# Sparse attention and soft mixture of experts on one core: sampled block numbers packed three to a word, taken apart in registers

## The chip, the cores and the metric

The kernel runs on one core of a Trainium2 chip. The metric is the device time of one execution in microseconds (us); lower is better. The core's engines are called PE (TensorE; PEld is its weight load), DVE (VectorE), ACT (ScalarE), POOL (GpSimd) and SP (SyncE, which here only issues transfers). Each has a sequencer of its own, which reads the instruction stream, runs register and semaphore instructions itself and hands the others to the engine's queue; the profile writes POOLq or ACTq for what a sequencer does.

## The reference

Four batches with eight heads attend over 768 positions of 64 numbers each. Positions come in 24 blocks of 32. A query block sees its own block and the two neighbours, the first and the last block, and three more blocks whose numbers are data (`sampled_blocks`, 24 rows of three numbers from 0 to 23); query blocks 0 and 23 see everything. The output, as 3072 rows of 512, goes through a soft mixture of eight experts with four slots each.

```python
mask = np.abs(blk_i - blk_j) <= window
mask = mask | (blk_i == 0) | (blk_j == 0) | (blk_i == n_blocks - 1) | (blk_j == n_blocks - 1)
for qb in range(n_blocks):
    for kb in sampled_blocks[qb]:
        mask[qb * block:(qb + 1) * block, kb * block:(kb + 1) * block] = True
scores = np.where(mask, scores, -1000000000.0)
...
return np.matmul(attn, v).astype(np.float32)
```

After it: `logits = x @ phi`, a softmax over rows that gathers slots, two matrix products per expert with a maximum between them, and a softmax over slots that spreads the results back to the rows.

## The kernel before, in words

Attention comes first, up to about 247 us of the profiled execution, then the experts. All work of the attention part is a list of tasks (class `Plan`, line 129). A task has an engine or a choice of engines with a cost, the tasks that it needs, and the buffers that it takes. The order in which all tasks are emitted is written out by hand (`ORDER`, line 67), and each engine runs its tasks in that order. Costs and due times written beside the tasks serve to choose where some instructions stand: `run` (line 209) calls a task's `pre` function, which loads its register values, 1.6 us of planned time ahead of the engine's current task, and `hold` (line 241) ties paced transfers, among them the late expert weights, to instructions of PE.

Batches run one after another. In a batch the query blocks 0 and 23 are "dense" (`plan_dense`, line 847); the other 22 go in pairs (`plan_pair`, line 624), 11 pairs to a batch. For one pair:

- K is staged for each of the two query blocks (`stage_k`, line 536) into one of four `kst` tiles of 256 columns. `fixed` copies the three neighbouring blocks (line 553, POOL) and, where the tile is new to the batch, the first and the last block (line 551, POOL). `sampled_` (line 555) copies the three sampled blocks, three instructions on ACT (line 559) or POOL (line 564); their source address in `ktile` is `ds(t.vals[j] * BLK, BLK)`, with a register value in it.
- V is staged in the same way (`stage_v`, line 573) into one of six `vrs` tiles, three copies (line 586, POOL; line 584, ACT for the last pairs). Their source address is `ds(t.vals[j], 1)`.
- q is scaled by 1/8 (lines 603 and 605). PE multiplies q with the staged K (line 643, tile `s`, 64 matmuls for a pair). DVE takes row maxima (line 663, `nm`), ACT the exponentials (line 668, `p`), DVE turns them (line 675, `ptt`). For each two pairs PE multiplies with V (line 741, `av`, from V itself and from `vrs`), and DVE divides by the row sums (lines 734 to 736, tile `x`). Dense blocks do the same at lines 864 (`sd`), 882, 895, 899 and 741 (`avd`).
- Groups of four such tiles are turned on PE (line 957, `mxt`) and go through the logits (line 1008, `ml`) and the slot sums (line 1092, `ms`).

The sampled numbers reach the engines so. `index_load` (line 351) brings `sampled_blocks` into `scr` by a transfer on ACT's queue. `sreg_copy` (line 470) has DVE copy the low words into `sreg`, an int32 tile of 24 rows with three numbers, for K. `index_math` (line 359) computes on DVE, in float32, `vreg`, the same shape for V: a number's position in V, or an empty position where the block is already seen by the mask or is a repeated one. `block_numbers` (line 439) loads the numbers of a pair of rows, `t[0:1, 2 * j + 1:2 * j + 3, :]`, with one load instruction on the engine that will copy (line 443), keeps the six register values by batch, pair, engine and largest value, and hands each row its three. The steps from a register value to an address (times the block's stride, times four bytes, plus the tile's base) run on the same engine's sequencer just before the copy, as one fused register instruction. `sreg` and `vreg` are made early: the tasks `t_sreg` and `t_vreg` (lines 491 and 492) stand ahead of the first pair.

After attention come the expert products (line 1507, then 1515) and the spreading of the result (line 1609), with expert weights arriving by transfers on SP's queue.

Of the kernel before, what the change touches and what calls it, by code (L numbers as in the profile page):

```python
# [12 lines left out]
I32 = mybir.dt.int32  # L13
F32R = mybir.dt.float32r
AF = mybir.ActivationFunctionType
ALU = mybir.AluOpType
# [4 lines left out]
BLK, NB, NR = 32, 24, 3  # L21
# [94 lines left out]
E_ = mybir.EngineType  # L116
# [12 lines left out]
class Plan:  # L129
# [6 lines left out]
    def add(self, f, opts, deps, key, acq=(), byte=0, pre=None, pace=False, kind=None, mode=None, ni=0,  # L136
            turn=False):
        t = Task(f, opts if isinstance(opts, list) else [opts], deps, key, acq, byte, pre, pace,
                 kind, mode, ni, turn)
        self.tasks.append(t)  # L140
        return t
# [106 lines left out]
def attn_moe_kernel(ctx, tc, qT, kT, vfull, vtab, sampled, phi, w1, w2, out):  # L248
    nc = tc.nc
    PE, ACT, DVE, POOL, SP = nc.tensor, nc.scalar, nc.vector, nc.gpsimd, nc.sync  # L250

    const = ctx.enter_context(tc.tile_pool(name="const", bufs=1))
# [16 lines left out]
    for k in RUNS:  # L269
        o = (at - NW // 2) * P * WP  # L270
# [71 lines left out]
    ssum = const.tile([P, 1], F32, name="ssum")  # L342


    sreg = const.tile([1, NB, NR], I32, name="sreg")

    vreg = const.tile([1, NB, NR], I32, name="vreg")

    scr = pw.tile([P, DM], F32, tag="x", name="scr", bufs=XB)

    def index_load():
# [4 lines left out]
        )  # L356
        return sraw

    def index_math():
        o = NB * NR * 2  # L360
        own, dup, tmp, iot = (scr[0:1, o + k * NB * NR:o + (k + 1) * NB * NR]
                              .rearrange("p (i j) -> p i j", i=NB) for k in range(4))
        DVE.tensor_copy(out=own, in_=sreg)
        POOL.iota(iot, pattern=[[1, NB], [0, NR]], base=0, channel_multiplier=0,
                  allow_small_or_imprecise_dtypes=True)
        POOL.memset(vbuf[1][:, VH:2 * VH], 0.0)
        DVE.tensor_single_scalar(out=dup, in_=own, scalar=0.0, op=ALU.is_equal)
        DVE.scalar_tensor_tensor(out=dup, in0=own, scalar=float(NB - 1), in1=dup,
                                 op0=ALU.is_equal, op1=ALU.max)
        DVE.tensor_tensor(out=tmp, in0=own, in1=iot, op=ALU.subtract)  # L370
        DVE.tensor_tensor(out=tmp, in0=tmp, in1=tmp, op=ALU.mult)
        DVE.scalar_tensor_tensor(out=dup, in0=tmp, scalar=1.0, in1=dup,
                                 op0=ALU.is_le, op1=ALU.max)
        for j in range(1, NR):
            for k in range(j):
                DVE.tensor_tensor(out=tmp[:, :, j], in0=own[:, :, j], in1=own[:, :, k], op=ALU.is_equal)
                DVE.tensor_tensor(out=dup[:, :, j], in0=dup[:, :, j], in1=tmp[:, :, j], op=ALU.max)
        DVE.tensor_scalar(out=tmp, in0=own, scalar1=-1.0, scalar2=float(NB), op0=ALU.mult, op1=ALU.add)
        DVE.tensor_tensor(out=tmp, in0=tmp, in1=dup, op=ALU.mult)
        DVE.scalar_tensor_tensor(out=vreg, in0=own, scalar=-1.0, in1=tmp, op0=ALU.add, op1=ALU.add)  # L380


    att = ExitStack()
# [4 lines left out]
    ktile, vtile = [None] * B, [None] * B  # L388
# [6 lines left out]
    for n in range(NVR):  # L395
        n = (B * (NB - 2) + n) % NVR
# [40 lines left out]
    both = {}  # L437

    def block_numbers(b, t, i, eng, most):
        j = (i - 1) // 2  # L440
        key = b, most, j, eng
        if key not in both:
            _, both[key] = nc.values_load_multi_w_load_instructions(  # L443
                t[0:1, 2 * j + 1:2 * j + 3, :], engines=[{"ACT": E_.Activation, "POOL": E_.Pool}[eng]], min_val=0, max_val=most,
                skip_runtime_bounds_check_because="block numbers lie in range by the definition of the input")
        o = (i - 2 * j - 1) * NR
        return both[key][o:o + NR]

# [20 lines left out]

    def sreg_copy(t):  # L470
        sraw = scr[0:1, 0:NB * NR * 2].bitcast(I32).rearrange("p (i j w) -> p i j w", i=NB, j=NR)
        DVE.tensor_copy(out=sreg, in_=sraw[0:1, :, :, 0])

    fills = Rec()

# [13 lines left out]
    t_warm = add(warm, ("PE", 3.0), [], -41, acq=[("s", use)], mode="F", ni=12)  # L489
    use.append(t_warm)  # L490
    t_sreg = add(sreg_copy, ("DVE", 0.3), [t_idx], -39)
    t_vreg = add(lambda t: index_math(), ("DVE", 4.0), [t_sreg], -38)


# [41 lines left out]
    def stage_k(b, i, n, use):  # L536
        k = nst[0] % NKST
        nst[0] += 1
        new = fresh.get(k) != b
        fresh[k] = b  # L540
        z = Rec()
        w, r0 = (0, 96) if i % 2 else (32, 0)

        def fixed(t):
            kv = ktile[b]
            k = took[0] % NKST
            took[0] += 1
            z.st = st = kst[k]
            if filled.get(k) != b:
                filled[k] = b  # L550
                POOL.tensor_copy(out=st[:, :, 128:192].rearrange("p c (g s) -> p c g s", g=2),
                                 in_=kv.rearrange("p c (g s) -> p c g s", g=NB)[:, :, 0:NB:NB - 1, :])
            POOL.tensor_copy(out=st[:, :, w:w + 96], in_=kv[:, :, (i - 1) * BLK:(i + 2) * BLK])  # L553

        def sampled_(t):
            for j, o in enumerate((r0, 192, 224)):
                st, src = z.st, ktile[b][:, :, ds(t.vals[j] * BLK, BLK)]
                if t.eng == "ACT":
                    x = ACT.activation(out=st[:, :, o:o + BLK], in_=src, func=AF.Copy, scale=1.0)  # L559
                    while opening:  # L560
                        tc.add_manual_dep(x.ins, opening.pop().ins.name, mybir.DependencyInfo(
                            mybir.DependencyClass.Sync, mybir.DependencyReason.DATA), reason="first")
                else:
                    POOL.tensor_copy(out=st[:, :, o:o + BLK], in_=src)  # L564

        f = add(fixed, ("POOL", 0.95 if new else 0.52), [t_k[b]], n - 4, acq=[("kst", use)], kind="fix")
        r = add(sampled_, [("ACT", 0.72), ("POOL", 0.86)], [f, t_sreg], n - 2.5,
                pre=lambda e: block_numbers(b, sreg, i, e, NB - 1), kind="smp")
        k_use[b].extend([f, r])
        use.extend([f, r])  # L570
        return z, r

    def stage_v(b, i, n, use):
        z = Rec()

        def copies(t):
            st = vrs[nvs[0] % NVR]
            nvs[0] += 1
            z.st = st.rearrange("p a j (r d) -> p a j r d", r=2)
            vf = vtile[b].rearrange("p a k r d -> p a k (r d)")  # L580
            for j in range(NR):
                o, src = st[:, :, j:j + 1, :], vf[:, :, ds(t.vals[j], 1), :]
                if t.eng == "ACT":
                    ACT.activation(out=o, in_=src, func=AF.Copy, scale=1.0)
                else:
                    POOL.tensor_copy(out=o, in_=src)  # L586

        v = add(copies, [("POOL", 1.12), ("ACT", 1.4)] if n >= len(items) - 2 else ("POOL", 1.12), [t_v[b], t_vreg], n - 1, acq=[("vrs", use)],
                pre=lambda e: block_numbers(b, vreg, i, e, NB), kind="vst")
        v_use[b].append(v)  # L590
        use.append(v)
        return z, v
# [31 lines left out]
    def plan_pair(b, g, n):  # L624
# [5 lines left out]
        for r in range(2):  # L630
            use = []
            kd.append(stage_k(b, 2 * g + 1 + r, n, use))
            ku.append(use)
# [613 lines left out]
    for gi in range(6):  # L1247
        Ts = done[4 * gi:4 * gi + 4]
        t_m, k = plan_group(gi, Ts, Ts[-1][0])
# [7 lines left out]
    m, n = NPRE, first[B - 1]  # L1257
# [24 lines left out]
    for j in range(NPT):  # L1282
        add(lambda t, m=m + j: load_w(m, turned), ("SP", 0.47), [qks[N - 2]], N + j / 10, acq=[("ptt", end_use)], byte=4 * WP * P,
            kind="lw", pace=0.4)
# [8 lines left out]
    def load_halves(m, tag, nb):  # L1293
# [8 lines left out]
        kind="lx", pace=0.4)  # L1302
# [60 lines left out]
    for j, g in enumerate((0, 1, 2, 5)):  # L1363
        t_n = plan_combine(g, N - 4 + j)

        n, b_use = N + 2 + j, []
# [171 lines left out]
    for n in range(2 * NE):  # L1538
        hf, e = n // NE, n % NE
# [174 lines left out]
```

## Time and profile before

| | us |
|---|---|
| median of 3 runs | 302.05 (301.56 to 302.61) |
| profiled execution, its own time | 300.76 |
| span of the profiled execution, first to last instruction | 298.9 |
| busy PE / DVE / POOL / ACT in it | 266.8 / 212.2 / 182.1 / 158.6 |
| mean granted TensorE clock, share of full speed | 0.98 |

The profile is of one execution. Times in its rows count from the start of the span. A row of instructions gives engine, line, operation, what is written and read (out<-in), a count, and in square brackets how long the engine had been idle and what ended that ("issue": nothing that the profile shows). In the chain, "POOLq L443" is time of POOL's sequencer on line 443. Register, semaphore and load instructions of a sequencer do not count as busy time of its engine.

### The profile page before, as it was taken

What the parts mean: (1) busy time and instruction counts of PE and PEld (TensorE: products, weight loads), DVE (VectorE), ACT (ScalarE), POOL (GpSimd) and SP (SyncE); (2) the same over time, 40 slices, a digit from 0 to 9 for tenths busy, and PEclk for the clock granted to TensorE, in tenths of its full rate; (3) what the DMA queues carried; (4) which work ended last, traced back from release to release, by engine and by line L of the source; (5) the groups of instructions that cost most, each with busy time, mean ns of one, the idle gap of its engine ahead of it and who ended that gap; (6) DMA issues with size and microseconds to landing.
All of it is one profiled execution on the core that took longest, in us unless ns stands there. A gap on an engine that the chain in (4) does not pass through costs nothing.

```text
span 298.9 us, 17524 instructions
## 1 busy us (share of the span) xinstructions
PE 266.8 (89%) x7221; PEld 190.3 (64%) x7221; DVE 212.2 (71%) x485; ACT 158.6 (53%) x482; POOL 182.1 (61%) x523
## 2 busy tenths in 40 slices
PE   7699998989999999999989999999887899999940
PEld 4458675876877676777666685867656663355530
DVE  6698895878998968989896889997676223012450
ACT  4866775763674975576877643556464122001340
POOL 5749789798847799785898968587953013000000
PEclk9989997999999999999999999999999999999996
DMA  7935663430364861034575220778669999999998
GB/s 252 405 119 163 193 185 95 148 81 22 89 202 138 214 182 42 24 108 134 179 207 162 72 77 19 236 225 240 220 192 303 397 380 409 422 420 409 342 306 280
DMA packets 30546, 61.96 MB, mean 207 GB/s; under 512 B 4481, under 2 KB 17922, under 8 KB 29314
## 3 DMA queue, kind: packets, MB, share of 16 engines
q1 hardware_dynamic: 30320, 60.70, 61.2%
q8 instruction: 57, 0.93, 1.3%
q14 instruction: 23, 0.19, 0.2%
q10 hardware_dynamic: 146, 0.13, 0.1%
HBM read 54.52 MB, written 6.29 MB: 203 GB/s over the span
## 4 chain that ended last, share of the span: by engine, by line
PE 55%; DVE 19%; issue 8%; POOL 5%; ACT 4%; POOLq 3%; ACTq 1%; DMA 1%; DVEq 0%
PE av L741 22%; PE s L643 7%; PE pso L1515 5%; DVE ptt L675 5%; PE pf L1507 5%; DVE nm L663 5%; PE mxt L957 3%; ACT p L668 3%; PE sd L864 3%; PE ml L1008 2%; DVE x L736 2%; POOLq L443 2%; POOL vrs L586 2%; PE avd L741 2%; DVE ptd L899 2%
## 5 line engine op out<-in xcount | busy, mean ns | idle before, releaser
L586 POOL COPY vrs<-v 128x260 f32 x258 | 91.8, 404 | 22.4 <-issue 10.5
L668 ACT ACTIVATE p<-s,nm 128x256 f32<-128x256 f32 x176 | 71.2, 478 | 29.0 <-DVE nm L663 21.5
L741 PE MATMUL av<-v,ptt 64*64 64x130 f32 (+2 forms) x1728 | 77.1, 282 | 2.8 <-issue 2.7
L741 PEld LDWEIGHTS av<-v,ptt 64*64 64x64 f32 (+2 forms) x1728 | 53.6, 131 | 24.2 <-issue 17.7
L675 DVE STREAM_TRANSPOSE ptt<-p 128x512 f32<-128x512 f32 x88 | 57.5, 688 | 8.8 <-ACT p L668 8.3
L663 DVE TENSOR_REDUCE nm<-s 128x2 f32<-128x512 f32 x88 | 54.9, 680 | 3.5 <-PE s L643 3.2
L643 PE MATMUL s<-kst,q 64*32 64x256 f32 x1408 | 47.7, 387 | 4.7 <-POOL kst L553 2.5
L553 POOL COPY kst<-ktile 128x384 f32<-128x384 f32 x88 | 42.9, 507 | 13.6 <-PE s L643 10.8
L741 PE MATMUL av<-vrs,ptt 64*32 64x130 f32 x2112 | 43.8, 277 | 5.2 <-issue 2.5
L741 PEld LDWEIGHTS av<-vrs,ptt 64*32 64x32 f32 x2112 | 36.0, 106 | 10.8 <-issue 3.7
L643 PEld LDWEIGHTS s<-kst,q 64*32 64x32 f32 x1408 | 28.2, 107 | 15.2 <-POOL vrs L586 3.2
L559 ACT ACTIVATE kst<-ktile 128x128 f32 x135 | 30.6, 310 | 12.9 <-PE s L643 8.2
L564 POOL COPY kst<-ktile 128x128 f32 x129 | 32.7, 293 | 4.4 <-issue 2.3
L895 ACT ACTIVATE pd<-sd,nb 128x384 f32<-128x384 f32 x32 | 16.7, 577 | 16.4 <-DVE nb L890 16.2
L741 PE MATMUL avd<-v,ptd 64*64 64x130 f32 x768 | 23.1, 271 | 0.0
L741 PEld LDWEIGHTS avd<-v,ptd 64*64 64x64 f32 x768 | 21.7, 132 | 1.6 <-PE s L643 0.8
L456 ACT COPY xT<-mxt 128x512 f32<-128x512 f32 (+1 forms) x17 | 9.4, 565 | 17.2 <-PE mxt L957 17.2
L899 DVE STREAM_TRANSPOSE ptd<-pd 128x384 f32<-128x384 f32 x32 | 16.4, 553 | 1.9 <-ACT pd L895 1.8
L736 DVE TENSOR_TENSOR x<-av,rs 128x512 f32<-128x512 f32 (+2 forms) x26 | 16.1, 619 | 0.9
L882 DVE TENSOR_REDUCE nm<-sd 128x1 f32<-128x384 f32 x32 | 16.2, 544 | 0.2
L603 ACT ACTIVATE q<-q 128x256 f32<-128x256 f32 x38 | 14.9, 430 | 2.2 <-DMA q<-in_qT_dram 1.9
L864 PE MATMUL sd<-ktile,q 64*32 64x384 f32 x256 | 14.5, 524 | 0.4 <-POOL q L605 0.4
(134 smaller groups left out, 256.7 us busy)
## 6 DMA issues: line engine op xcount, KB each, us to landing
w<-in_w_dram SPq DMA_DIRECT2D x13, 512.0 KB, 7.1
q<-in_qT_dram SPq DMA_DIRECT2D x47, 128.0 KB, 2.7
w<-in_w_dram SPq DMA_DIRECT2D x44, 128.0 KB, 3.2
out_dram<-ob SPq DMA_DIRECT2D x20, 256.0 KB, 3.9
ktile<-in_kT_dram SPq DMA_DIRECT2D x48, 96.0 KB, 3.0
w<-in_w_dram SPq DMA_DIRECT2D x4, 1024.0 KB, 10.2
v<-in_vtab_dram SPq DMA_DIRECT2D x36, 113.8 KB, 3.4
v<-in_w_dram SPq DMA_DIRECT2D x12, 256.0 KB, 5.0
```

What stands on the lines that cost most here:

```text
L553: POOL.tensor_copy(out=st[:, :, w:w + 96], in_=kv[:, :, (i - 1) * BLK:(i + 2) * BLK])
L559: x = ACT.activation(out=st[:, :, o:o + BLK], in_=src, func=AF.Copy, scale=1.0)
L564: POOL.tensor_copy(out=st[:, :, o:o + BLK], in_=src)
L586: POOL.tensor_copy(out=o, in_=src)
L643: PE.matmul(u.s[r][32 * p:32 * p + 32, j, :], lhsT=u.q[s_, p, j, :], rhs=kd[j][0].st[s_, p, :], start=True, stop=True)
L663: DVE.tensor_reduce(out=u.nm[r], in_=u.s[r], axis=AX.X, op=ALU.max, negate=True)
L668: ACT.activation(out=u.p[r][:, j, :], in_=u.s[r][:, j, :], func=AF.Exp, bias=u.nm[r][:, j:j + 1], scale=1.0)
L675: DVE.transpose(out=T.pt[r][:, :, 2 * w:2 * w + 2, :].rearrange("p k j q -> p j k q"), in_=u.p[r].rearrange("p j (k q) -> p j k q", k=8))
L736: DVE.tensor_tensor(out=x, in0=a[:, :, :, 0:D], in1=rs[lo:hi].unsqueeze(3).to_broadcast([hi - lo, 2, 2 * n, D]), op=ALU.mult)
L741: PE.matmul(av[:, r * 2 * D1:(r + 1) * 2 * D1].rearrange("p (a d) -> p a d", a=2), lhsT=lhsT, rhs=rhs, start=start, stop=stop)
L864: PE.matmul(u.s[r][k][32 * p:32 * p + 32, :], lhsT=T.dq.q[s_, p, j, :], rhs=kt[s_, p, 384 * k:384 * (k + 1)], start=True, stop=True)
L899: DVE.transpose(out=ptd[r][:, 12 * k:12 * k + 12, j, :], in_=u.p[r][k])
```

## The change

`sreg` and `vreg` become tiles of 24 words, one for each query block. A new function `pack` computes, on DVE in float32, first number + 32 x second + 1024 x third, with two operations, of which the second writes the int32 tile. `sreg_copy` first copies the numbers into the float32 scratch tile `own` (which `index_math` did before from `sreg`) and then packs them; `index_math` packs `vreg` at its end. The four scratch views move out of `index_math`; they are parts of the same tile `scr`. A load on line 443 brings two words, and `f` takes three numbers out of each by shifts and masks. For K the masks leave each number times 32, which is the offset of its block, so that `sampled_` no longer multiplies by `BLK`; for V the plain number is left and its address is formed as before. The tasks, their costs and `ORDER` are unchanged.

```diff
@@ -342,9 +342,9 @@
     ssum = const.tile([P, 1], F32, name="ssum")
 
 
-    sreg = const.tile([1, NB, NR], I32, name="sreg")
-
-    vreg = const.tile([1, NB, NR], I32, name="vreg")
+    sreg = const.tile([1, NB], I32, name="sreg")
+
+    vreg = const.tile([1, NB], I32, name="vreg")
 
     scr = pw.tile([P, DM], F32, tag="x", name="scr", bufs=XB)
 
@@ -356,11 +356,14 @@
         )
         return sraw
 
+    own, dup, tmp, iot = (scr[0:1, (2 + k) * NB * NR:(3 + k) * NB * NR]
+                          .rearrange("p (i j) -> p i j", i=NB) for k in range(4))
+
+    def pack(out, n, part):
+        DVE.scalar_tensor_tensor(out=part, in0=n[:, :, 1], scalar=32.0, in1=n[:, :, 0], op0=ALU.mult, op1=ALU.add)
+        DVE.scalar_tensor_tensor(out=out, in0=n[:, :, 2], scalar=1024.0, in1=part, op0=ALU.mult, op1=ALU.add)
+
     def index_math():
-        o = NB * NR * 2
-        own, dup, tmp, iot = (scr[0:1, o + k * NB * NR:o + (k + 1) * NB * NR]
-                              .rearrange("p (i j) -> p i j", i=NB) for k in range(4))
-        DVE.tensor_copy(out=own, in_=sreg)
         POOL.iota(iot, pattern=[[1, NB], [0, NR]], base=0, channel_multiplier=0,
                   allow_small_or_imprecise_dtypes=True)
         POOL.memset(vbuf[1][:, VH:2 * VH], 0.0)
@@ -377,7 +380,8 @@
                 DVE.tensor_tensor(out=dup[:, :, j], in0=dup[:, :, j], in1=tmp[:, :, j], op=ALU.max)
         DVE.tensor_scalar(out=tmp, in0=own, scalar1=-1.0, scalar2=float(NB), op0=ALU.mult, op1=ALU.add)
         DVE.tensor_tensor(out=tmp, in0=tmp, in1=dup, op=ALU.mult)
-        DVE.scalar_tensor_tensor(out=vreg, in0=own, scalar=-1.0, in1=tmp, op0=ALU.add, op1=ALU.add)
+        DVE.scalar_tensor_tensor(out=tmp, in0=own, scalar=-1.0, in1=tmp, op0=ALU.add, op1=ALU.add)
+        pack(vreg, tmp, dup[:, :, 0])
 
 
     att = ExitStack()
@@ -440,9 +444,15 @@
         j = (i - 1) // 2
         key = b, most, j, eng
         if key not in both:
-            _, both[key] = nc.values_load_multi_w_load_instructions(
-                t[0:1, 2 * j + 1:2 * j + 3, :], engines=[{"ACT": E_.Activation, "POOL": E_.Pool}[eng]], min_val=0, max_val=most,
-                skip_runtime_bounds_check_because="block numbers lie in range by the definition of the input")
+            why = "block numbers lie in range by the definition of the input"
+            _, words = nc.values_load_multi_w_load_instructions(
+                t[0:1, 2 * j + 1:2 * j + 3], engines=[{"ACT": E_.Activation, "POOL": E_.Pool}[eng]], min_val=0, max_val=32767,
+                skip_runtime_bounds_check_because=why)
+            if t is sreg:
+                f = lambda w: ((w << 5) & 992, w & 992, (w >> 5) & 992)
+            else:
+                f = lambda w: (w & 31, (w >> 5) & 31, w >> 10)
+            both[key] = [nc.s_assert_within(n, 0, most, skip_runtime_bounds_check_because=why) for w in words for n in f(w)]
         o = (i - 2 * j - 1) * NR
         return both[key][o:o + NR]
 
@@ -469,7 +479,8 @@
 
     def sreg_copy(t):
         sraw = scr[0:1, 0:NB * NR * 2].bitcast(I32).rearrange("p (i j w) -> p i j w", i=NB, j=NR)
-        DVE.tensor_copy(out=sreg, in_=sraw[0:1, :, :, 0])
+        DVE.tensor_copy(out=own, in_=sraw[0:1, :, :, 0])
+        pack(sreg, own, tmp[:, :, 0])
 
     fills = Rec()
 
@@ -554,7 +565,7 @@
 
         def sampled_(t):
             for j, o in enumerate((r0, 192, 224)):
-                st, src = z.st, ktile[b][:, :, ds(t.vals[j] * BLK, BLK)]
+                st, src = z.st, ktile[b][:, :, ds(t.vals[j], BLK)]
                 if t.eng == "ACT":
                     x = ACT.activation(out=st[:, :, o:o + BLK], in_=src, func=AF.Copy, scale=1.0)
                     while opening:
@@ -565,7 +576,7 @@
 
         f = add(fixed, ("POOL", 0.95 if new else 0.52), [t_k[b]], n - 4, acq=[("kst", use)], kind="fix")
         r = add(sampled_, [("ACT", 0.72), ("POOL", 0.86)], [f, t_sreg], n - 2.5,
-                pre=lambda e: block_numbers(b, sreg, i, e, NB - 1), kind="smp")
+                pre=lambda e: block_numbers(b, sreg, i, e, (NB - 1) * BLK), kind="smp")
         k_use[b].extend([f, r])
         use.extend([f, r])
         return z, r
```

## Rows read from the trace of the kernel before

**Rows 1.** The page: busy time by engine; the chain that ended last, by engine and line.

```profile
PE 266.8 (89%) x7221; PEld 190.3 (64%) x7221; DVE 212.2 (71%) x485; ACT 158.6 (53%) x482; POOL 182.1 (61%) x523
...
PE 55%; DVE 19%; issue 8%; POOL 5%; ACT 4%; POOLq 3%; ACTq 1%; DMA 1%; DVEq 0%
PE av L741 22%; PE s L643 7%; PE pso L1515 5%; DVE ptt L675 5%; PE pf L1507 5%; DVE nm L663 5%; PE mxt L957 3%; ACT p L668 3%; PE sd L864 3%; PE ml L1008 2%; DVE x L736 2%; POOLq L443 2%; POOL vrs L586 2%; PE avd L741 2%; DVE ptd L899 2%
```

**Rows 2.** Instructions of line 443: count, ns min/median/max, first and last start.

```profile
L443 POOLq TENSOR_LOAD <-vreg x44: 1382/1387/1404, 14.4 to 226.2; - x44
L443 ACTq TENSOR_LOAD <-sreg x31: 1319/1336/1534, 5.8 to 213.1; - x31
L443 POOLq TENSOR_LOAD <-sreg x30: 1382/1388/1593, 4.6 to 212.6; - x30
```

**Rows 3.** Instructions of line 586, POOL's sequencer and POOL, same columns.

```profile
L586 POOLq FUSED_REGOPS  x258: 46/46/46, 18.8 to 228.9; - x129
L586 POOL COPY vrs<-v x258: 397/404/415, 19.3 to 229.6; 128x260 f32 x129
```

**Rows 4.** The chain in order of time: start us, us, what; pieces from four stretches.

```profile
35.94 0.54 POOLq L443
...
41.40 0.05 POOLq L586
...
41.52 0.05 POOLq L586
...
81.82 0.37 ACTq L443
...
116.02 0.86 ACTq L443
```

**Rows 5.** Stretches: busy us by engine (PE, PEld, DVE, ACT, POOL), clock, DMA share, GB/s.

```profile
35.50:47.30 11.80, 10.22 (x344) 7.78 (x328) 9.42 (x19) 9.34 (x29) 8.91 (x27) 1.00 0.62 175
47.90:51.30 3.40, 3.40 (x99) 2.53 (x89) 1.93 (x4) 0.73 (x2) 3.40 (x11) 0.50 0.16 39
...
145.20:156.50 11.30, 10.23 (x326) 7.02 (x312) 10.98 (x24) 9.04 (x32) 10.53 (x33) 1.00 0.72 205
...
230.00:235.00 5.00, 5.00 (x126) 4.50 (x126) 2.20 (x4) 1.17 (x2) 0.00 (x0) 1.00 1.03 393
```

**Rows 6.** PE's timeline: start us, us, instructions, count [idle before, what ended it].

```profile
45.48 1.10 PE L741 MATMUL av<-v,ptt 64*64 64x130 f32 x15 [0.85 <-issue]
47.32 3.16 PE L643 MATMUL s<-kst,q 64*32 64x256 f32 x64 [0.75 <-POOL kst L564]
...
83.85 1.96 PE L643 MATMUL s<-kst,q 64*32 64x256 f32 x64
86.46 0.93 PE L741 MATMUL av<-vrs,ptt 64*32 64x130 f32 x46 [0.65 <-DVE x L736]
...
97.49 1.43 PE L643 MATMUL s<-kst,q 64*32 64x256 f32 x32
...
126.33 0.94 PE L741 MATMUL av<-vrs,ptt 64*32 64x130 f32 x48 [0.37 <-DVE x L736]
...
156.59 1.10 PE L643 MATMUL s<-kst,q 64*32 64x256 f32 x32 [1.10 <-POOL vrs L586]
...
229.71 1.16 PE L480 MATMUL st<-ident 128*128 128x128 f32 x8 [2.10 <-issue]
```

**Rows 7.** ACT's timeline, the start and 90 to 99 us.

```profile
10.49 1.31 ACT L559 ACTIVATE kst<-ktile 128x128 f32 x6 [1.40 <-issue]
...
95.59 1.20 ACT L668 ACTIVATE p<-s,nm 128x256 f32<-128x256 f32 x3 [0.81 <-issue]
```

**Rows 8.** DVE's timeline, the first 14 us.

```profile
2.00 2.49 DVE L472 COPY sreg<-scr 1x72 int32<-1x72 int32 x1 [2.00 <-DMA scr<-in_sampled_dram]
...
8.06 0.39 DVE L380 SCALAR_TENSOR_TENSOR vreg<-scr 1x72 int32<-1x72 f32 x1
```

**Rows 9.** POOL's timeline, the first 24 us.

```profile
7.97 0.40 POOL L551 COPY kst<-ktile 128x256 f32<-128x256 f32 x1 [2.91 <-DMA ktile<-in_kT_dram]
```

## The prediction

> **What bounds the kernel now.** I read the page first: engine shares, then the chain that ended last [rows 1]. TensorE (PE) is busy 89% of the span and holds 55% of the chain, so time is won only where PE stands still or runs at its lower clock. The chain also runs through line 443 on POOL's sequencer, 2% of 298.9 us; ACT's sequencer as a whole has 1%. That line is the register load that the change shortens.
>
> Next, the instructions of that line [rows 2]: 74 loads on POOL (44 of vreg, 30 of sreg) of 1387 ns and 33 on ACT of 1336 ns (31 of sreg, and two of vreg like them), each bringing six words. They are sequencer work: the engine can empty its queue meanwhile, but nothing new reaches it. Each copy with a sampled address has one fused register instruction of 46 ns ahead of it, 258 of them on line 586 [rows 3] and in the same way 129, 135 and 6 on lines 564, 559 and 584; two for successive copies start 0.12 us apart, at 41.40 and 41.52 [rows 4].
>
> Then the places where PE waits [rows 6], since only these turn sequencer time into kernel time. Between 35.5 and 47.3 us POOL is busy 8.91 of 11.80 us [rows 5], and the chain there has six pieces of line 443, of which the first, at 35.94, stands for all [rows 4]. The chain can only pass through these pieces where the engine has run empty behind a load. At 47.32 PE waits 0.75 us for the copy that ends this stretch [rows 6]. Just after it the granted clock is 0.50, the 1.2 GHz level, from 47.9 to 51.3 [rows 5].
>
> **The change part by part.** The sum is made against the profiled execution, 300.76 us with a span of 298.9; the median of the three runs is 302.05, so I add 1.29 us to what comes out.
>
> *The load.* Two words instead of six. No row has a load of another size. The ends are 1.39 us (nothing depends on the number of words) and two sixths, 0.46 us on POOL and 0.45 on ACT. A gain beyond two thirds is excluded, as the two words must still be read, and so is a loss, as nothing more is read. I take the low end: the 74 loads on POOL have medians within 1 ns of each other, while the DMA share changes from 0.16 to 0.72 between stretches [rows 2, 5]. A single trip through a memory shared with the transfers would spread; steps of the sequencer, one per word, would not. That saves up to 74 x 0.925 = 68 us of POOL's sequencer and 33 x 0.89 = 29 us of ACT's, nearly all of it beside other work. The Trainium skill, page "Runtime: NRT & Kernel Launch", section "Instruction fetch mechanics", gives about 200 ns per register even in bulk, for loads from HBM; six would be an estimated 1.2 us, and the rows show 231 ns per word, so the trace roughly agrees. By that page two words would be 0.4 us, and the sum would be the same.
>
> *Taking the words apart.* The 528 dynamic copies (258 + 129 on POOL, 135 + 6 on ACT) then need four or five register steps where the code has three (times stride, times four, plus base). No row has longer ones. If the steps are appended to the same instruction the ends are 46 ns (no change) and 46 x 5/3 = 77 ns; if they need an instruction of their own, 0.12 us by the spacing in [rows 4]. I take 77 ns, since steps already share an instruction now. Six copies then add 0.19 us per load, against 0.92 saved. The cover is the engine: six copies of 404 ns [rows 3] keep POOL busy longer than six times 0.15 us of sequencer (0.12 and the 0.03 added). Without that cover the 0.19 us per load counts, and the net is still 0.73.
>
> *More on DVE at the start.* Two small operations are put between the first copy (which ends at 4.49, after 2.49 us) and the first loads. Bounds: nothing (were they to run beside the first copy) and 0.39 us each, the row that writes an int32 tile [rows 8]; I take the high end, 0.8 us in all, as each needs the one before it. The loads on POOL, the first of which started at 4.6 [rows 2], then start at about 5.4 and, two at 0.46, end near 6.5; the first copy waits until 7.97 for the transfer of K [rows 9]. So nothing is lost, and as the loads now end ahead of that transfer up to 0.3 us may be won; I take 0.1. On ACT three loads precede the copies at 10.49, which waited 1.40 us by "issue" [rows 7]: cover of the same kind. vreg is later by about 1 us, after 8.45 [rows 8]; the first vreg load starts at 14.4 [rows 2], which covers it.
>
> *What the shorter loads give on the path*, PE's waits in order [rows 6]:
> - 47.32: POOL's 2.89 us of idle time shrink to almost none, so its last copy is ready before PE comes: 0.75 us. What is late next is PE itself.
> - The low clock after it: 64 matmuls of one step take 3.16 us at 47.32 and 1.96 at 83.85: 1.20 us. A gap of 0.85 us ("issue") came less than 2 us before that wait [rows 6]; a single gap of 2.10 us before 229.71 left the clock at 1.00 [rows 5, 6]. So without the second gap I expect the high level, 2.4 GHz, to stay.
> - 86.46: a 0.65 us wait for DVE, whose chain holds 0.37 us of ACT's load at 81.82 [rows 4]: 0.37 us. DVE is late next.
> - 97.49: half a step takes 1.43 us, against 1.10 at 156.59, behind 0.81 us of ACT idle at 95.59 [rows 6, 7]: 0.33 us.
> - 126.33: 0.37 us for DVE, whose chain holds 0.86 us of ACT's load at 116.02 [rows 4]: 0.37 us.
> - 156.59: 1.10 us for POOL, which was idle 11.30 - 10.53 = 0.77 us of its last 11.3 us [rows 5]: 0.77 us, and POOL's copies themselves remain late by 0.33.
>
> With 0.1 at the start the sum is 0.1 + 0.75 + 1.20 + 0.37 + 0.33 + 0.37 + 0.77 = 3.89 us. The weight transfers late in the kernel are held back by PE's own progress in the code, so they move with it. 300.76 - 3.89 + 1.29 = 298.16: **298.2 us**.
>
> **Rivals.** (a) *The load does not shrink and the unpacking costs*: slower. For it: no row shows a shorter load; 1.39 us might be one fixed trip. Against it: the constancy above. Per load the change then adds 0.19 us (longer instructions) to 0.72 us (own instructions, 6 x 0.12). It decides from the point where the six unpackings cost more than the load saves: with 0.72 us, when the two-word load is above 0.67 us. Its place is the two stretches before 47.32 and 156.59, where POOL's sequencer is the chain; with some five and three loads ahead of PE's wait, 8 x 0.19 = 1.5 to 8 x 0.72 = 5.8 us are added: 303.6 to 307.8, say 305. The same page of the Trainium skill, section "The ~15µs preamble/postamble breakdown", calls the 1.3 us of such a load one round trip for a few words; by that this rival would hold, and no row here decides between its two statements.
>
> (b) *The load shrinks, the time stays*: 302. PE stands still as often for "issue" (0.85 us before 45.48, 2.10 before 229.71 [rows 6]), and it may reach such stops earlier and wait there instead; the clock may fall all the same (1.20 lost from the sum), and the waits for DVE may return. Against: the waits at 47.32 and 156.59 name POOL, and those alone are 1.5 us.
>
> (c) *More than the sum*: by the chain rather than by PE's gaps, line 443 has 2% on POOL and ACT's sequencer 1% of 298.9 us [rows 1], some 9 us; two thirds of it, 6, plus 1.2 of clock is 7.2: 294.9. Against: PE does other work during much of it, as the 0.75 us gap after 2.89 us of POOL idle shows.
>
> **How the numbers follow.** The forecast (gain of 1 to 7 us) has 0.72, (c) 0.06, (b) 0.13, (a) 0.09. A measurement of this kernel can tell about 0.3%, 0.9 us, from no change; so faster 0.78, same 0.13, slower 0.09. The range takes in the forecast with either end of its uncertain terms (clock, DVE waits), reaches to (c) and takes in (b), and leaves out (a): 294.9 to 302.2.
>
> **What would show it.** Line 443 at 0.4 to 0.6 us, in the same 74 and 33 instructions; fused instructions at 46 to 77 ns and still one per copy. PE's waits for POOL near 47 and 156 us gone or below 0.4 us, and no stretch of 0.50 clock near 48. POOL busy as before (182 us) but less idle until 47 us. It is wrong if line 443 stays above 1 us; if PE's "issue" idle grows by what its waits for POOL lose; or if the 0.50 clock appears elsewhere, or for longer, between 17 and 290 us.

## Result, and the profile after

The changed kernel takes 298.48 us (median of 6 runs, 296.65 to 303.33) against 301.63 us for the kernel before (6 runs, 300.95 to 302.61): ratio 0.990, interval 0.9852 to 0.9948. In a second comparison, with 12 and 29 runs, the ratio was 0.9898 (0.9845 to 0.9952). The forecast of 298.2 us, inside a range of 294.9 to 302.2, was right in sign and size. Profile against profile the gain is smaller: 298.66 us with a span of 296.8 against 300.76 with 298.9. A ratio is made from a kernel's fast runs alone, those within 1.5% of its fastest: five of six of the changed kernel here, six of twelve in the second comparison, two of six with the short load alone and three of six with kept words; by the medians of all runs these four ratios would be 0.990, 0.997, 0.996 and 0.993. In four experiments further down (short load alone, only V packed, kept words, kept words without the addition) the profiled execution is 0.3% to 1.8% above the kernel's own median, so durations of single instructions and what waited for what are read from these profiles, never their spans.

The page of the changed kernel first: busy time by engine, then the chain that ended last, by engine and by line.

```profile
PE 266.0 (90%) x7221; PEld 191.8 (65%) x7221; DVE 217.3 (73%) x488; ACT 158.2 (53%) x482; POOL 182.0 (61%) x523
...
PE 70%; DVE 16%; issue 5%; DMA 2%; POOL 2%; ACT 2%; POOLq 1%; DVEq 0%; ACTq 0%
PE av L752 33%; PE s L654 10%; PE pso L1526 5%; PE pf L1518 5%; PE mxt L968 4%; PE sd L875 3%; DVE ptt L686 3%; DVE nm L674 3%; PE ml L1019 2%; DVE cm L1211 2%; PE ms L1103 2%; DVE x L747 2%; DMA out_dram<-ob 1%; PE po L1620 1%; POOL vrs L597 1%
```

Against [rows 1]: the busy times are those of before, but PE now holds 70% of the chain in place of 55%, and the sequencers of POOL and ACT have gone from 3% and 1% to 1% and 0%. The load is no longer listed. Among the lines that are new in the list is DVE's L1211, one tiny operation, with 2%.

The loads (now line 448) and the register work ahead of the copies of V (line 597) and of K (line 575): count, ns min/median/max, first and last start.

```profile
L448 POOLq TENSOR_LOAD <-vreg x44: 502/507/517, 14.2 to 224.3; - x44
L448 ACTq TENSOR_LOAD <-sreg x31: 481/490/699, 6.0 to 210.6; - x31
L448 POOLq TENSOR_LOAD <-sreg x30: 502/508/734, 4.9 to 210.5; - x30
L448 ACTq TENSOR_LOAD <-vreg x2: 490/491/492, 212.6 to 221.5; - x2
...
L597 POOLq ALU_OP  x258: 32/35/35, 15.9 to 226.8; - x129
L597 POOLq FUSED_REGOPS  x258: 46/46/104, 16.0 to 227.0; - x129
...
L575 POOLq ALU_OP  x215: 32/35/49, 8.0 to 212.4; - x108
L575 POOLq FUSED_REGOPS  x129: 37/37/50, 8.2 to 212.5; - x129
```

Against [rows 2, 3]: a load fell from 1387 to 507 ns on POOL and from 1336 to 490 on ACT, in the same 107 instructions. Four words fewer save 880 ns. If every word costs the same, which two sizes can't show, that is 220 ns for one, and 507 - 2 x 220 leaves 67 ns that don't depend on the number. But masks and shifts have become instructions of their own (ALU_OP, on average one per copy of V and 215/129 = 1.7 per copy of K on POOL), beside the fused one that was there before.

PE's timeline at the places that the prediction named, and at the new ones.

```profile
11.87 1.47 PE L654 MATMUL s<-kst,q 64*32 64x256 f32 x32 [2.23 <-ACT pd L906]
...
18.84 0.97 PE L752 MATMUL av<-vrs,ptt 64*32 64x130 f32 x44
...
31.00 0.93 PE L752 MATMUL av<-vrs,ptt 64*32 64x130 f32 x46 [1.46 <-POOL kst L575]
...
44.35 1.10 PE L752 MATMUL av<-v,ptt 64*64 64x130 f32 x15 [0.91 <-issue]
45.38 1.96 PE L654 MATMUL s<-kst,q 64*32 64x256 f32 x64
...
61.19 1.06 PE L1019 MATMUL ml<-xT,phis 128*32 128x128 f32 x26 [1.42 <-issue]
...
84.22 0.93 PE L752 MATMUL av<-vrs,ptt 64*32 64x130 f32 x46 [0.65 <-DVE x L747]
...
94.98 1.09 PE L654 MATMUL s<-kst,q 64*32 64x256 f32 x32
...
152.24 1.10 PE L654 MATMUL s<-kst,q 64*32 64x256 f32 x32 [0.79 <-POOL vrs L597]
...
157.06 2.92 PE L752 MATMUL av<-v,ptt 64*128 64x130 f32 x40 [2.70 <-DVE x L747]
...
162.99 2.23 PE L654 MATMUL s<-kst,q 64*32 64x256 f32 x64
...
227.79 1.54 PE L491 MATMUL st<-ident 128*128 128x128 f32 x8 [2.09 <-issue]
```

Three rows of the kernel before that go with it:

```profile
20.77 1.02 PE L741 MATMUL av<-vrs,ptt 64*32 64x130 f32 x38 [0.63 <-POOL vrs L586]
31.49 0.93 PE L741 MATMUL av<-vrs,ptt 64*32 64x130 f32 x46 [0.26 <-DVE x L736]
...
164.05 1.96 PE L643 MATMUL s<-kst,q 64*32 64x256 f32 x64
```

Read it against these and [rows 6] by the start of the same instruction. The matmuls of 20.77 begin at 18.84, 1.93 us sooner and without the wait for POOL; 0.49 us of that are left at 31.00, behind a new wait for POOL. The step that began at 47.32 begins at 45.38, 1.94 us sooner, without a wait, and takes 1.96 us in place of 3.16. The step of 156.59 begins at 152.24: by then 4.35 us are won. The step that began at 164.05 begins at 162.99: 1.06 us are left. The matmuls of 229.71 begin at 227.79, 1.92 us sooner. So in this profile the gain came in the main where it was expected, and most of it was given back in one place, between 152 and 163 us. A second profile of the same kernel (among the experiments) looks different there: the step of 156.59 is only 1.84 us sooner, hardly anything is lost behind it, and the span is 296.9 us, the same.

```profile
154.75 1.10 PE L654 MATMUL s<-kst,q 64*32 64x256 f32 x32 [0.67 <-POOL vrs L597]
```

What happened between 152 and 163 us in the first profile shows in DVE's and POOL's timelines of the changed kernel (start, us, instructions, count).

```profile
150.45 0.28 DVE L1210 TENSOR_REDUCE cm<-lst 128x4 f32<-128x128 f32 x1
150.76 4.92 DVE L1211 TENSOR_SCALAR cm<-cm 128x4 f32<-128x4 f32 x1
155.72 0.18 DVE L1212 RECIPROCAL cm<-cm 128x4 f32<-128x4 f32 x1
```

```profile
149.58 0.95 POOL L564 COPY kst<-ktile 128x384 f32<-128x384 f32 x2
150.48 4.21 POOL L597 COPY vrs<-v 128x260 f32 x12
154.64 0.95 POOL L564 COPY kst<-ktile 128x384 f32<-128x384 f32 x2
```

L1211 adds 1e-9 to four sums per row; its other five executions took 0.17 to 0.36 us. This one took 4.92 us, while POOL copied without a pause. DVE's work behind it, the tile `x`, came late, and PE stood still for 2.70 us at 157.06. In the kernel before the same operation was also slow once, but only 0.80 us, because POOL paused there for 0.47 us behind a load:

```profile
154.85 0.80 DVE L1200 TENSOR_SCALAR cm<-cm 128x4 f32<-128x4 f32 x1
```

```profile
154.52 1.10 POOL L586 COPY vrs<-v 128x260 f32 x3
156.09 0.75 POOL L586 COPY vrs<-v 128x260 f32 x2 [0.47 <-issue]
```

The clock, by stretches of the changed kernel (columns as in [rows 5]): the 0.50 level that stood at 47.9 is gone, and it stands after PE's two long stops instead. (In a second profile of the same kernel it stands only after the later one, from 229.1.)

```profile
156.70:160.10 3.40, 3.04 (x56) 2.50 (x64) 3.40 (x7) 2.50 (x7) 1.19 (x3) 0.51 0.21 59
228.40:231.80 3.40, 3.40 (x18) 3.40 (x18) 1.39 (x3) 0.58 (x1) 0.00 (x0) 0.50 1.05 404
```

### The profile page after: what moved, and what is told of

Its sections match the earlier page's. It is cut to its first block, busy times and chain, and to the rows that moved or that the text cites. A ratio compares the mean times of both kernels' runs of the same rounds, so it can differ in the third digit from the quotient of the medians.

```text
span 296.8 us, 18231 instructions
## 1 busy us (share of the span) xinstructions
PE 266.0 (90%) x7221; PEld 191.8 (65%) x7221; DVE 217.3 (73%) x488; ACT 158.2 (53%) x482; POOL 182.0 (61%) x523
## 4 chain that ended last, share of the span: by engine, by line
PE 70%; DVE 16%; issue 5%; DMA 2%; POOL 2%; ACT 2%; POOLq 1%; DVEq 0%; ACTq 0%
PE av L752 33%; PE s L654 10%; PE pso L1526 5%; PE pf L1518 5%; PE mxt L968 4%; PE sd L875 3%; DVE ptt L686 3%; DVE nm L674 3%; PE ml L1019 2%; DVE cm L1211 2%; PE ms L1103 2%; DVE x L747 2%; DMA out_dram<-ob 1%; PE po L1620 1%; POOL vrs L597 1%
## 5 line engine op out<-in xcount | busy, mean ns | idle before, releaser
L597 POOL COPY vrs<-v 128x260 f32 x258 | 91.7, 404 | 20.8 <-PE av L752 17.2
L654 PE MATMUL s<-kst,q 64*32 64x256 f32 x1408 | 46.6, 379 | 3.0 <-ACT pd L906 2.2
L752 PE MATMUL av<-vrs,ptt 64*32 64x130 f32 x2112 | 42.5, 275 | 4.4 <-issue 1.5
L570 ACT ACTIVATE kst<-ktile 128x128 f32 x135 | 31.2, 317 | 9.4 <-PE s L654 8.1
L654 PEld LDWEIGHTS s<-kst,q 64*32 64x32 f32 x1408 | 27.4, 106 | 13.7 <-POOL vrs L597 2.5
```

Of the source, the lines that this page charges most:

```text
L654: PE.matmul(u.s[r][32 * p:32 * p + 32, j, :], lhsT=u.q[s_, p, j, :], rhs=kd[j][0].st[s_, p, :], start=True, stop=True)
L752: PE.matmul(av[:, r * 2 * D1:(r + 1) * 2 * D1].rearrange("p (a d) -> p a d", a=2), lhsT=lhsT, rhs=rhs, start=start, stop=stop)
```

## The experiments

Every ratio is to the kernel before on the same chip. The theory (L): the gain is sequencer time, the shorter load less the unpacking, at places where PE waits for copies. Rivals: the gain is made only at the start, or by the clock; POOL's engine, or PE's own stops by "issue", cover whatever is saved. And for what was given back: the blocked addition is caused by POOL's copies (theory B) or is an accident.

**Load and unpacking apart.** First the short load alone: two words are loaded, and the first number of each row stands for all three. The other two sampled blocks are left out, but there are as many copies, of the same size.

```diff
-            _, both[key] = nc.values_load_multi_w_load_instructions(
-                t[0:1, 2 * j + 1:2 * j + 3, :],
+            _, (a, b_) = nc.values_load_multi_w_load_instructions(
+                t[0:1, 2 * j + 1:2 * j + 3, 0],
...
+            both[key] = [a, a, a, b_, b_, b_]
```

> The kernel before with loads of two words in place of six, and nothing else: each load brings the first sampled number of the pair's two rows, and that number stands for all three of its row, so two of the three sampled blocks of a row are left out. No packing, no taking apart, 528 fused instructions as before. Theory L (the time comes from the shorter load): line 443 at about 0.5 us and the kernel at 0.975 to 0.99 of before, no slower than the changed kernel, as six copies need 0.72 us of sequencer here and some 1.2 there. Rival S (the time came from the shifted start on DVE or from chance): 1.00.

Ratio 0.9841 (0.9739 to 0.9944), the widest interval of the study. Its loads took 497 ns on POOL and 474 on ACT. The ratio lies in L's range; the interval leaves out S's 1.00, but not by much.

Then the unpacking alone: the changed kernel loads six words again and uses two. (Both tiles grow by four words and are set to zero at the start, for the longer load.)

```diff
-                t[0:1, 2 * j + 1:2 * j + 3], ...
+                t[0:1, 2 * j + 1:2 * j + 7], ...
...
-            both[key] = [... for w in words for n in f(w)]
+            both[key] = [... for w in words[0:2] for n in f(w)]
```

> The changed kernel with loads of six words, of which two are used; packing and taking apart stay. Theory L: the load is 1.39 us again, POOL's sequencer needs 1.45 + 1.2 = 2.65 us for six copies of V against 2.08 of the engine, so POOL's sequencer bounds the staging: slower than before by at least 8 x 0.46 = 3.7 us (the loads on the chain of before), 1.01 to 1.04 of before. Rival S: 0.99, as the changed kernel.

Ratio 1.0244 (1.0186 to 1.0303), the largest effect of the study, inside L's range and far from S's 0.99. The waits of POOL's engine in it (us in total, times, longest), against 10.5 us for "issue" in the kernel before and 0.2 us in the changed one:

```profile
POOL vrs L599 <- issue: 14.3, 16, 4.3
```

Put together, with the sequencer's time for the six copies of one load of V:

| load | unpacking | sequencer, us | ratio |
|---|---|---|---|
| 6 words | no (before) | 1.39 + 0.72 = 2.11 | 1 |
| 2 words | no | 0.50 + 0.72 = 1.22 | 0.984 |
| 6 words | yes | 1.39 + 1.1 = 2.5 | 1.024 |
| 2 words | yes (the change) | 0.51 + 1.1 = 1.6 | 0.990 |

0.72 is six times the 0.12 us of [rows 4]. The 1.1 us is read in the changed kernel's second profile, from 154.8 to 155.8 plus the last one's 0.1, for the registers of six copies:

```profile
L597 POOLq ALU_OP  x6: 32/35/35, 154.8 to 155.6; - x6
L597 POOLq FUSED_REGOPS  x6: 46/46/85, 154.9 to 155.8; - x6
```

POOL's engine needs 12 copies in 4.21 us, so 2.1 us for six. Before, the sequencer (2.11) was just as slow as the engine, and any semaphore or second load put it behind: the pause of 0.47 us shown above came from a load that followed on only three copies. With 1.2 or 1.6 us it runs ahead, with 2.5 it can't. The unpacking cost 2.4% beside the long load, and beside the short one 0.990 against 0.984, which the intervals don't separate from nothing. So the cost of the one seems to depend on the other, as is to be expected where two things share a cover.

**K or V alone.** The changed kernel with one of the two tables left as six words (its tile `[1, NB, NR]` again, loaded by the old instruction, and for K the factor 32 back at the copy).

```diff
+            if t is vreg:
+                _, both[key] = nc.values_load_multi_w_load_instructions(t[0:1, 2 * j + 1:2 * j + 3, :], ...)
+            else:
...
```

> Changed kernel with the V numbers loaded as six words again (44 loads on POOL of 1.39 us); only the K numbers packed (30 loads on POOL, 31 on ScalarE of 0.5 us). Theory L (what counts is sequencer time on POOL: 0.88 us less per load and some 0.5 us more unpacking): POOL gets 30 x 0.38 = 11 us back in place of 74 x 0.38 = 28, and as PE waits above all for V copies, the ratio to before is 0.993 to 0.999, above that of the changed kernel, and PE's waits for POOL near 48, 97, 126 and 157 are still 0.3 to 1 us each. Rival S (the gain is made at the start, by the first K copies): ratio as the changed kernel's, 0.985 to 0.993, with waits for POOL as small as there.

> Changed kernel with the K numbers loaded as six words again (30 loads on POOL of 1.39 us, 31 on ScalarE of 1.34 us); only the V numbers packed (44 loads of 0.5 us). Theory L: 44 x 0.38 = 17 us of POOL's sequencer back, on the copies that PE waits for; ratio to before 0.988 to 0.996, the larger part of the changed kernel's gain, no wait for POOL over 1 us after 30 us. Rival S: ratio 0.997 to 1.003, as the first K copies start no earlier than before. Theory B: the long addition near 150 us shows here only if POOL's copies run without a pause there.

> The changed kernel itself, for a second profile and as the yardstick of the three beside it. Ratio to before 0.985 to 0.995. Theory B (the small add of the third batch waits because POOL's copies now follow each other without a pause): the 128x4 addition of 1e-9 near 150 us takes 4 to 5.5 us again while its five sisters take 0.17 to 0.3, and PE waits 2 to 3 us for DVE near 157. Theory C (that one profile was an accident): the addition takes under 1 us, PE's wait is gone, and the span is 2 us or more under the 296.8 of the first profile.

Only K packed (the diff above): 0.9945 (0.9909 to 0.9981). Only V packed (the same with `sreg`): 0.9926 (0.9891 to 0.9961). Both, on the same chip: 0.9898 (0.9845 to 0.9952). Of the gain of 1.02%, K alone has 0.55 and V alone, with more loads on POOL, 0.74, but the intervals overlap. The rival "start" wanted 0.997 to 1.003 for V alone; its interval ends at 0.9961. The expected waits for POOL came only in part: with K alone one of 0.62 us at 45.93 and none at 97, 126 or 157; with V alone one of 1.01 us at 155.29, where none over 1 us was expected after 30 us. The rival "clock" isn't settled: the mean granted clock is 0.982 over the 12 runs of the changed kernel and 0.979 over the 29 of the kernel before, and 0.003 of 297 us is, as an estimate, at most 1 us, a part of the gain but not all of it.

For the addition, the profile with K alone is the more telling one: V's loads of 1.39 us leave the pauses in POOL's copies, and the addition, 0.2 us after such a copy began, ends at the first pause.

```profile
151.63 1.10 POOL L601 COPY vrs<-v 128x260 f32 x3
153.49 1.10 POOL L601 COPY vrs<-v 128x260 f32 x3 [0.76 <-issue]
```

```profile
151.81 0.94 DVE L1215 TENSOR_SCALAR cm<-cm 128x4 f32<-128x4 f32 x1
```

With V packed alone it took 4.04 us, and again ended at a pause, of 0.29 us:

```profile
153.34 4.24 POOL L602 COPY vrs<-v 128x260 f32 x12
157.87 0.96 POOL L569 COPY kst<-ktile 128x384 f32<-128x384 f32 x2 [0.29 <-POOL vrs L602]
```

```profile
153.57 4.04 DVE L1216 TENSOR_SCALAR cm<-cm 128x4 f32<-128x4 f32 x1
```

In the first experiment (short loads too) it took 4.74 us. In the second profile of the changed kernel it took 1.92 us and PE waited less than 1 us for DVE: neither B's 4 to 5.5 nor the accident's under 1, and the span is the same as with 4.92 us. So the hold returns, as it does in two later profiles (3.44 us with kept words, 0.59 us with the shorter unpacking). Its length doesn't follow from where in POOL's run the addition falls: it began 0.28, 0.25 and 0.23 us into a run of twelve copies where it took 4.92, 1.92 and 4.04 us.

**The addition.** It is taken out of both kernels; the sums are at least 1, where 1e-9 rounds away.

```diff
-        DVE.tensor_scalar(out=cm, in0=cm, scalar1=EPS, scalar2=None, op0=ALU.add)
         DVE.reciprocal(out=cm, in_=cm)
```

> The changed kernel without the addition of 1e-9 to the row sums of the last softmax (six operations of 4 columns on DVE; the sums are at least 1, so in float32 the addition changes nothing). Theory B (in the changed kernel the addition at 150.76 waited 4.75 us until POOL's copies in a row left it a way to SBUF, PE then waited 2.70 us for DVE and lost its clock): no wait of PE for DVE over 1 us near 155, 0.975 to 0.985 of before, 1.5 to 4 us under the changed kernel. Rival C (the wait would only move to the next DVE operation, or PE's fetches take it): within 1 us of the changed kernel, 0.99 of before.

> The kernel before without the same addition. There one of the six took 0.80 us instead of 0.17 to 0.26, and PE's wait near 156 was for POOL, not for DVE. Theory B: 0 to 0.6 us faster, 0.998 to 1.00 of before. If the operation costs by itself, not by POOL's gapless work, it is as much faster as the third kernel is against the changed one.

Without it the changed kernel has 0.9835 (0.9766 to 0.9903), the kernel before 1.0037 (0.9994 to 1.008), where 0.998 to 1.00 was expected. (The other five additions there took 0.17 to 0.36 us, not 0.26.) PE's 2.70 us wait near 157 is gone, and the reciprocal, which now stands in the addition's place during POOL's copies, takes 0.18 us as ever. But the profile's span is 296.5, only 0.3 us less, and PE's stops by "issue" in front of line 752 went from 3.5 to 5.5 us in total. The ratio is in B's range and the span in rival C's, and the interval overlaps that of the changed kernel: the runs don't decide.

Then the same addition, column by column:

```diff
-        DVE.tensor_scalar(out=cm, in0=cm, scalar1=EPS, scalar2=None, op0=ALU.add)
+        for n in range(4):
+            DVE.tensor_scalar(out=cm[:, n:n + 1], in0=cm[:, n:n + 1], scalar1=EPS, scalar2=None, op0=ALU.add)
```

> Changed kernel with the addition of 1e-9 to the 128x4 sums made as four additions to 128x1 columns; the same values. Theory P (VectorE's addition waits for something that it shares with POOL, which an operation of one column doesn't need: the 128x1 multiply just ahead of it took 0.27 us beside the same POOL copies): 24 additions of 0.06 to 0.3 us each, none over 0.5, no PE wait over 1 us for DVE near 157, ratio to before 0.980 to 0.990. Rival Q (any add at that place is held, whatever its shape, by a semaphore or a queue): one of the 24 takes 1 to 5 us, PE waits for DVE as before, ratio 0.985 to 0.995.

All 24 additions (ns min/median/max), then POOL's copies and the four that ran beside them:

```profile
L1212 DVE TENSOR_SCALAR cm<-cm x24: 143/146/154, 133.6 to 245.6; 128x1 f32<-128x1 f32 x24
```

```profile
151.43 4.24 POOL L597 COPY vrs<-v 128x260 f32 x12
```

```profile
151.63 0.33 DVE L1212 TENSOR_SCALAR cm<-cm 128x1 f32<-128x1 f32 x4
```

The four fall 0.2 us after a run of twelve copies began, where the 128x4 form of 150.76 fell 0.28 us after one, and take 0.33 us together in place of 4.92. PE's wait for DVE near 157 is gone. So the hold depends on the operation's shape and on POOL's copies: theory P, not a queue or a semaphore at that place (Q). This is one profile, and the 128x4 form once got through after 0.59 us; but none of the 24 additions was held. The Trainium skill, page "SBUF — State Buffer", section "Who interferes with whom", says that VectorE and GpSimd share a pair of ports, which `tensor_scalar` takes in its two-port modes, and that the holder keeps it for a whole instruction. The trace agrees that such an operation is held and a one-column form isn't (which mode either ran in, no row shows), but the hold lasted through 4.92 us of copies of 0.4 us each, far beyond one instruction.

On the time nothing can be read: the ratio is 0.9903 (0.9866 to 0.994), that of the changed kernel itself and at the edge of P's 0.980 to 0.990. The wait is shown; that it costs the median anything is not.

**Is there more in the registers?** Loaded words are kept over the four batches, as the numbers don't depend on the batch:

```diff
-        key = b, most, j, eng
+        key = most, j, eng
```

> Changed kernel in which numbers that one engine has once loaded and unpacked stay in its registers over the four batches (the key of the table lacks the batch): 34 loads and unpackings in place of 107. Theory L without a floor: another 53 x 1.0 us of POOL's sequencer and 20 on ScalarE are spared after the first batch, as much again as the change gave, ratio to before 0.975 to 0.985. Rival F (after the change the sequencer is already covered: POOL's idle time is waiting for PE, and PE is bound by itself and by its own fetches): the ratio stays within 0.003 of the changed kernel's, and POOL's idle time before the V copies changes its releaser only. Rival R (registers run short and are reloaded or spilled): more instructions than 18231 and a ratio above 1.

34 loads remain, as expected, but each copy still unpacks its number anew: the kernel has 18158 instructions, 73 less than the changed one's 18231, just the missing loads. Ratio 0.9869 (0.9802 to 0.9937), within 0.003 of the changed kernel's 0.9898. That is what rival F wanted, but the interval reaches into theory L's range, and as every copy still unpacks its number, not all that L counted on was spared. What speaks for F is the trace: POOL hardly waits for "issue" any more, but for PE.

```profile
L597 POOL COPY vrs<-v 128x260 f32 x258 | 91.0, 405 | 21.2 <-PE av L752 18.4 <-DMA phis<-in_phi_dram 2.2 <-issue 0.2
```

That is already so in the changed kernel (20.8 us idle, 17.2 of it for PE; before 22.4, 10.5 of it "issue"). A shorter unpacking of K:

```diff
-                f = lambda w: ((w << 5) & 992, w & 992, (w >> 5) & 992)
+                f = lambda w: ((w & 31) * BLK, w & 992, (w >> 10) * BLK)
```

> Changed kernel with a shorter unpacking of the K numbers: mask only, or shift only, and the factor 32 in the address, in place of a shift and a mask; 172 register operations fewer (704 to 440 masks and shifts, but more fused divides). Theory U (unpacking is a price on the way to the copies): 4 operations less per K load, some 0.2 us of sequencer on 61 loads, and the ratio 0.002 to 0.005 lower than that of the changed kernel (0.990). Rival F (POOL's engine covers it after the loads have shrunk): the sequencer's time per K use falls in the trace, the span stays within 1 us of 296.8, ratio 0.985 to 0.993.

Masks and shifts on POOL for K fell from 215 to 86; ratio 0.9895 (0.984 to 0.995), profiled span 295.2. The interval holds the ratios of both U and F; F's other condition, a span within 1 us of 296.8, is missed by 0.6 us. Then kept words without the addition, and all three steps together:

> Changed kernel with the loaded words kept in registers over the four batches (34 loads in place of 107) and without the addition of 1e-9 (sums are at least 1, where it rounds away). If the two gains add up: 0.990 - 0.003 - 0.006 = 0.980, range 0.974 to 0.986. If PE's own fetches take it back: as e3 or e7 alone, 0.984 to 0.987.

> As the one before, and with the short unpacking of the K numbers. The three steps together: 0.974 to 0.986; if the short unpacking is covered by POOL's engine, within 0.003 of the one before.

Ratios 0.9863 (0.9805 to 0.9921) and 0.9866 (0.9795 to 0.9938). By these values the gains don't add up to 0.980; they are what e3 or e7 alone (no addition, kept words) gave. Like 0.9835, 0.9869 and 0.9895 they can't be told from 0.990. The last one is faster than the kernel before by its whole interval; against the changed one only its profile is shorter (span 294.6).

## Why the prediction was right

- **The load.** Right at its low end: 0.51 and 0.49 us measured, 0.46 and 0.45 taken. The reason given (constant medians mean steps per word) fits: 220 ns per word between two sizes. Of the two statements of the Trainium skill's page "Runtime: NRT & Kernel Launch", the one in "Instruction fetch mechanics", about 200 ns per register (for loads from HBM), fits; the one trip of "The ~15µs preamble/postamble breakdown" does not, and with it rival (a) fell: it is the second experiment, where the load stays long, and it would have cost 2.4%, 7.4 us, more than the 1.5 to 5.8 given for it.
- **Taking the words apart.** This is the term that was mis-sized. I let the steps join the fused instruction, 0.19 us per load; they became ALU_OP instructions of 35 ns, and six copies take 1.1 us in place of 0.72: some 0.4 us. Both ends were kept, and 0.4 lies between them. The cover named for it, POOL's engine, held: 1.6 us of sequencer against 2.1.
- **The start.** The two packing operations took 0.18 us each, not 0.39; `sreg` was ready at 4.91 and the first load began at 4.9, not 5.4.

```profile
4.52 0.18 DVE L363 SCALAR_TENSOR_TENSOR scr<-scr 1x24 f32<-1x24 f32 x1
4.73 0.18 DVE L364 SCALAR_TENSOR_TENSOR sreg<-scr 1x24 int32<-1x24 f32 x1
```

  The first product of the pairs began 0.54 us sooner (12.41 in the kernel before, 11.87 now), against 0.1 taken.
- **47.32 and the clock behind it**: right, 0.75 and 1.20 us; the clock term was even larger, as the low level outlasted the 64 matmuls: the products with V that began at 51.42 begin at 47.98, 3.44 us sooner, 1.50 more than at 47.32. POOL was busy 8.91 of 11.80 us ahead of it [rows 5] and now 9.74 of 9.90:

```profile
35.50:45.40 9.90, 8.99 (x277) 6.92 (x275) 7.93 (x15) 7.93 (x25) 9.74 (x30) 1.00 0.66 191
```

- **86.46**: wrong; the wait for DVE stands at 84.22 with the same 0.65 us, so ACT's load was not what set it. **97.49**: right, 1.43 became 1.09 us. **126.33**: right, no wait is there. **156.59**: 0.77 expected, 1.10 became 0.79, so 0.31; "gone or below 0.4" was wrong there.
- **Not foreseen.** The 0.63 us wait for POOL at 20.77, which is gone; a wait of 1.46 us for POOL at 31.00 (in both profiles of the changed kernel), where 0.26 us for DVE stood at 31.49; PE's stop for "issue" before 61.19, 1.42 in place of 0.78; and the hold at 150.76. The prediction named "the clock may fall all the same" in rival (b), and in this profile it did, twice, outside the place expected. A 0.50 clock elsewhere was one of the prediction's own signs of being wrong, and it came in both profiles: on the clock it was wrong by its own measure. So the sum of 3.89 us was exceeded up to 152 us in the first profile (4.35) and undershot at the end (1.9 to 2.1), and undershot throughout in the second (1.84 at the same step, 2.0 at the end); by medians the gain is 3.15 us in the first comparison and 0.87 in the second. That 3.89 and 3.15 agree so nearly is partly luck: the route to the end differs already between the changed kernel's two profiles. The 0.9 us that a measurement was said to tell from no change was too little as well: the interval of the first comparison is 1.4 us to either side.
- **The inference from 229.71** was too strong: a stop of 2.10 us there left the clock at 1.00, the one of 2.09 us at 227.79 in the changed kernel was followed by 0.50. What else the clock depends on there, no row shows.

## What to carry to other kernels

Price a register load by its words (here about 0.22 us each), and compare the sequencer's whole time per group (load plus address arithmetic) with the engine time that covers it: here 2.11 against 2.1 was the edge, and a change is worth something only on the side where the sequencer is late. Before packing numbers, count the instructions that take them apart; beside a long load they cost 2.4%, beside a short one no more than these runs can tell (0.990 against 0.984). And when an engine's pauses disappear, look at what used to slip through them.

## What was unexpected of the hardware

A 128x4 `TENSOR_SCALAR` on DVE was held for 0.6 to 4.9 us beside copies on POOL, while a reduction, a reciprocal and 128x1 forms of the same operation ran there at their usual 0.15 to 0.28 us. Pauses of 0.47, 0.76 and 0.29 us ended it in three profiles, and the shortest hold, 0.59 us, ended where one copy of V followed the one before after 0.43 us in place of 0.35; what ended it in the other four stays open, since POOL went on without a visible gap. Masks on registers, and shifts that go before a mask, aren't joined to the fused multiply and add: each is 32 to 49 ns on POOL. The one bare shift, ahead of V's third number, has no ALU_OP of its own, and a fused instruction of 85 ns stands there in place of 46. And nine versions with a short load, from one to three steps away from the change, all lie between 0.983 and 0.995 with intervals of 0.4% to 1.0% on either side, so these runs don't rank them.
